# Superblock 0 ahead of superblock 1 in the head, weights issued behind GpSimd's products of superblock 1, and two output blocks in two steps each

## The chip, the core and the metric

The kernel runs on one core of one Trainium2 chip. A core has five engines with their own instruction queues: TensorE (PE in the profile, its weight loads PEld) for matrix products, VectorE (DVE), ScalarE (ACT) and GpSimd (POOL) for elementwise work, and SyncE (SP), which here only issues transfers. They meet through semaphores. The metric is the device time of one execution in microseconds; lower is better.

## What is computed

An RWKV-6 style recurrence over four batches of eight heads, 768 steps each, head size 48, whose output goes through an RMS norm and a gated feed-forward block (384 to 1536 to 384). Cut to what matters:

```python
# r, k, v, w: (4, 8, 768, 48); u: (8, 48)
state = 0                                   # (B, H, D, D)
for t in range(S):
    cur = einsum('bhd,bhe->bhde', u * k[t], v[t])
    y[t] = einsum('bhd,bhde->bhe', r[t], state + cur)
    state = w[t][..., None] * state + einsum('bhd,bhe->bhde', k[t], v[t])
x = y.transpose(0, 2, 1, 3).reshape(B * S, H * D)       # (3072, 384)
xn = x / sqrt(mean(x * x) + 1e-6) * rms_g
out = (silu(xn @ w_gate) * (xn @ w_val)) @ w_out        # 384 -> 1536 -> 384
```

## The kernel before

The 768 steps are cut into six superblocks of 128 steps. A step of the kernel is named fn.n.j: function, superblock n (0 to 5), and j, which is the batch (0 to 3) or, for the feed-forward steps, one of twelve blocks of 128 hidden units. Steps `load_gv.g.h` and `load_wo.g` take weight group g instead.

For each superblock and batch: `load_w`, `load_r`, `load_k`, `load_v` issue transfers on the sync queue (lines 247 to 261); `ln`, `cs_mm`, `exp_r`, `exp_k` make the running products of the decay w (logarithm on ACT, sums over steps on PE, exponentials on ACT); `r_mul` and `k_mul` scale r and k with them (lines 454 to 463; `k_mul` is on DVE in superblocks 0 and 1 and on POOL after that); `rk_pe` and `rk_tr` transpose the result (PE and an ACT copy in superblocks 0 and 1, a DMA transpose later); `q_mm` makes the 128x128 products of r and k, `q_mask_e`, `q_copy_o` and `q_mask_o` mask them; `bonus_mul` (two products on POOL, lines 467 and 468), `bonus_sum` (DVE) and `bonus_v` (POOL) make the term with u; `st_mm` and `st_new` carry the state; `x_pe`, `y_mm` or `y_mm`, `x_add` make y in PSUM; `x_sq`, `x_rstd`, `xn_mul`, `xn_pe`, `xn_out` are the norm and its transpose into `xnt`.

The feed-forward part of a superblock then takes twelve blocks of `gate_mm`, `val_mm` (three products of 512 columns each, line 626), `silu` (ACT) and `h_mul` (DVE, line 658), and four `o_mm` (twelve products of 384 columns each, line 672), `o_out` and `out_dma`. A hidden block's weights come from one of two tiles each for gate and value: group 0 holds blocks 0 to 3, group 1 blocks 4 to 11 (`GV = (0, 4, 12)`). The output weights `wo_sb` are one tile filled by three transfers of four blocks each (`load_wo.0` to `load_wo.2`, line 357). All weights are issued by POOL (lines 351 and 357), behind the POOL work that stands in front of them in the order.

The order of all work is written out by hand in the string `ORDER`: 1086 steps. Each engine runs its own steps in the order in which they stand there, and each queue its transfers. `warm` steps are products of zeros that PE does in the head, 36 of them.

PSUM has eight banks: two in ring "a" (gates, sums for r, y of even batches in superblock 0), two in ring "b" (values, sums for k, y of odd batches in superblock 0) and four in ring "q" (everything else). `psum` gives a new tile the bank of its ring whose last use stands earliest in `ORDER`, so the order of the steps also decides which bank a tile gets, and whom it waits for.

The next superblock's recurrence runs between the feed-forward blocks of the one before, so that PE has both to draw on; the head, up to the first `gate_mm.0.0`, has no feed-forward work to fill it.

Of the kernel before, what the change touches and what calls it, by code (L numbers as in the profile page):

```python
# [35 lines left out]
q_mm.0.2 load_r.2.0 q_mask_o.0.2 y_mm.0.1 bonus_mul.0.3 rk_tr.0.3 x_pe.0.0 q_mask_o.0.0 load_gv.0.0 q_mask_e.0.2
x_sq.0.1 cs_mm.1.1 y_mm.0.0 exp_r.1.1 load_w.2.3 bonus_v.0.2 warm.3.0 warm.20.0 bonus_sum.0.3 x_rstd.0.1 warm.15.0
x_sq.0.0 load_r.2.3 x_pe.0.2 y_mm.0.2 q_mm.0.3 warm.6.0 warm.14.0 xn_mul.0.1 bonus_v.0.3 warm.17.0 load_gv.0.1
x_rstd.0.0 r_mul.1.0 x_sq.0.2 warm.2.0 warm.33.0 warm.25.0 k_mul.1.0 xn_mul.0.0 load_gv.1.0 x_pe.0.3 warm.16.0
q_mask_e.0.3 q_mask_o.0.3 st_mm.0.0 warm.30.0 y_mm.0.3 exp_k.1.1 bonus_mul.1.0 bonus_mul.1.1 xn_pe.0.1 st_mm.0.3  # L40
x_rstd.0.2 st_new.0.0 warm.35.0 r_mul.1.1 warm.11.0 cs_mm.1.3 x_sq.0.3 warm.28.0 xn_pe.0.0 xn_out.0.1 xn_out.0.0
warm.0.0 st_new.0.3 xn_mul.0.2 x_rstd.0.3 exp_k.1.3 xn_mul.0.3 xn_pe.0.2 cs_mm.1.2 xn_out.0.2 xn_pe.0.3 xn_out.0.3
st_mm.0.2 rk_pe.1.0 st_mm.0.1 k_mul.1.1 exp_r.1.3 exp_r.1.2 st_new.0.2 exp_k.1.2 rk_tr.1.0 k_mul.1.3 gate_mm.0.0
val_mm.0.2 st_new.0.1 gate_mm.0.3 rk_pe.1.1 bonus_sum.1.0 silu.0.0 load_gv.1.1 val_mm.0.0 gate_mm.0.2 silu.0.3 silu.0.2
bonus_sum.1.1 rk_tr.1.1 h_mul.0.0 h_mul.0.2 r_mul.1.3 gate_mm.0.1 val_mm.0.3 gate_mm.0.9 silu.0.1 bonus_mul.1.3
val_mm.0.1 h_mul.0.3 silu.0.9 gate_mm.0.6 q_mm.1.0 bonus_sum.1.3 silu.0.6 gate_mm.0.7 q_copy_o.1.1 q_copy_o.1.0
q_mask_o.1.0 q_mask_o.1.1 gate_mm.0.5 rk_pe.1.3 bonus_v.1.0 h_mul.0.1 silu.0.7 val_mm.0.7 load_r.2.2 q_mask_e.1.0
load_wo.0.0 val_mm.0.6 q_mask_e.1.1 rk_tr.1.3 r_mul.1.2 gate_mm.0.11 k_mul.1.2 h_mul.0.7 cast_v.1.0 y_mm.1.0
load_wo.1.0 silu.0.5 cast_v.1.1 bonus_v.1.1 val_mm.0.9 rk_pe.1.2 h_mul.0.6 st_mm.1.0 st_mm.1.1 silu.0.11 val_mm.0.5
x_add.1.0 x_sq.1.0 h_mul.0.9 cast_v.1.2 val_mm.0.4 gate_mm.0.4 gate_mm.0.8 rk_tr.1.2 silu.0.4 st_new.1.0 st_new.1.1  # L50
q_mm.1.2 bonus_mul.1.2 load_wo.2.0 cast_v.1.3 q_copy_o.1.2 h_mul.0.5 silu.0.8 gate_mm.0.10 q_mask_o.1.2 h_mul.0.4
q_mask_e.1.3 val_mm.0.8 y_mm.1.1 st_mm.1.2 bonus_sum.1.2 q_copy_o.1.3 silu.0.10 bonus_v.1.3 st_mm.1.3 val_mm.0.11
q_mask_o.1.3 q_mask_e.1.2 h_mul.0.8 x_add.1.1 load_k.2.1 x_rstd.1.0 ln.2.0 x_sq.1.1 y_mm.1.3 h_mul.0.11 val_mm.0.10
bonus_v.1.2 x_add.1.3 y_mm.1.2 h_mul.0.10 x_rstd.1.1 x_add.1.2 xn_mul.1.0 x_sq.1.3 cs_mm.2.0 st_new.1.3 o_mm.0.0
x_rstd.1.3 ln.2.1 x_sq.1.2 load_v.2.1 xn_pe.1.0 cs_mm.2.1 ln.2.2 xn_mul.1.1 x_rstd.1.2 cs_add.2.0 xn_out.1.0 o_out.0.0
st_new.1.2 xn_mul.1.2 o_mm.0.2 cs_add.2.1 xn_pe.1.1 exp_r.2.0 r_mul.2.0 bonus_mul.2.0 exp_r.2.1 xn_pe.1.2 load_v.2.0
o_mm.0.1 w_tot.2.0 xn_out.1.2 cs_mm.2.2 exp_k.2.0 ln.2.3 xn_mul.1.3 w_tot.2.1 r_mul.2.1 load_k.2.2 load_k.2.3 exp_k.2.1
cs_mm.2.3 xn_out.1.1 xn_pe.1.3 cs_add.2.2 cs_add.2.3 k_mul.2.0 exp_r.2.2 o_mm.0.3 xn_out.1.3 k_mul.2.1 exp_r.2.3
cast_v.2.1 r_mul.2.2 bonus_mul.2.1 w_tot.2.2 o_out.0.2 exp_k.2.3 gate_mm.1.7 out_dma.0.0 val_mm.1.7 st_mm.2.1 rk_tr.2.0
exp_k.2.2 r_mul.2.3 w_tot.2.3 gate_mm.1.1 val_mm.1.1 k_mul.2.3 st_new.2.1 load_v.2.2 rk_tr.2.1 silu.1.7 gate_mm.1.5  # L60
k_mul.2.2 h_mul.1.7 silu.1.1 load_v.2.3 gate_mm.1.6 silu.1.5 val_mm.1.5 silu.1.6 h_mul.1.1 o_out.0.3 load_r.3.0
bonus_sum.2.1 load_w.3.1 bonus_mul.2.2 gate_mm.1.3 val_mm.1.6 o_out.0.1 gate_mm.1.0 h_mul.1.5 val_mm.1.0 bonus_sum.2.0
q_mm.2.0 silu.1.0 h_mul.1.6 cast_v.2.0 cast_v.2.2 val_mm.1.3 q_copy_o.2.0 q_mask_e.2.0 st_mm.2.0 q_copy_o.2.1 rk_tr.2.3
bonus_v.2.1 q_mask_o.2.0 h_mul.1.0 silu.1.3 st_new.2.0 q_mask_e.2.1 h_mul.1.3 gate_mm.1.2 st_mm.2.2 q_mask_o.2.1
silu.1.2 val_mm.1.2 y_mm.2.0 load_w.3.0 gate_mm.1.4 y_mm.2.1 gate_mm.1.10 bonus_v.2.0 rk_tr.2.2 h_mul.1.2 val_mm.1.4
silu.1.4 x_add.2.0 silu.1.10 x_add.2.1 st_new.2.2 gate_mm.1.9 gate_mm.1.8 val_mm.1.9 q_mm.2.2 h_mul.1.4 x_sq.2.1
x_sq.2.0 bonus_mul.2.3 load_r.3.1 silu.1.9 out_dma.0.3 gate_mm.1.11 cast_v.2.3 x_rstd.2.0 val_mm.1.11 x_rstd.2.1
load_k.3.0 bonus_sum.2.2 h_mul.1.9 q_mask_e.2.3 load_k.3.1 silu.1.8 load_v.3.0 q_copy_o.2.2 q_copy_o.2.3 q_mask_o.2.2
silu.1.11 ln.3.0 q_mask_e.2.2 load_w.3.3 q_mask_o.2.3 bonus_v.2.2 h_mul.1.11 load_w.3.2 ln.3.1 bonus_sum.2.3 st_mm.2.3
val_mm.1.10 y_mm.2.3 y_mm.2.2 val_mm.1.8 xn_mul.2.0 bonus_v.2.3 out_dma.0.2 h_mul.1.10 out_dma.0.1 load_r.3.3 cs_mm.3.0  # L70
x_add.2.2 h_mul.1.8 cs_add.3.0 o_mm.1.1 cs_mm.3.1 x_add.2.3 load_r.3.2 x_sq.2.2 load_v.3.2 load_k.3.2 st_new.2.3 ln.3.3
exp_r.3.0 x_sq.2.3 ln.3.2 x_rstd.2.2 w_tot.3.0 exp_k.3.0 xn_mul.2.2 xn_pe.2.0 xn_mul.2.1 cs_add.3.1 x_rstd.2.3 o_mm.1.0
xn_out.2.0 exp_r.3.1 exp_k.3.1 r_mul.3.0 o_out.1.0 k_mul.3.0 xn_pe.2.2 cs_mm.3.3 cs_add.3.3 k_mul.3.1 bonus_mul.3.1
w_tot.3.1 xn_mul.2.3 o_mm.1.3 rk_tr.3.0 xn_pe.2.1 xn_out.2.2 r_mul.3.1 bonus_mul.3.0 exp_r.3.3 o_out.1.1 out_dma.1.0
r_mul.3.3 cs_mm.3.2 cs_add.3.2 xn_pe.2.3 exp_k.3.2 rk_tr.3.1 w_tot.3.3 k_mul.3.2 exp_r.3.2 load_w.5.2 xn_out.2.3
xn_out.2.1 exp_k.3.3 r_mul.3.2 bonus_sum.3.1 load_k.4.2 o_out.1.3 o_mm.1.2 gate_mm.2.5 w_tot.3.2 val_mm.2.1
bonus_sum.3.0 o_out.1.2 bonus_v.3.0 cast_v.3.0 val_mm.2.0 cast_v.3.2 bonus_mul.3.2 out_dma.1.3 silu.2.5 gate_mm.2.0
q_mm.3.0 q_mask_e.3.0 load_k.3.3 silu.2.0 h_mul.2.0 load_v.3.1 gate_mm.2.1 silu.2.1 gate_mm.2.11 val_mm.2.5 h_mul.2.1
q_mask_e.3.1 silu.2.11 cast_v.3.1 rk_tr.3.2 st_mm.3.2 gate_mm.2.2 q_copy_o.3.0 k_mul.3.3 load_w.4.0 silu.2.2
q_copy_o.3.1 h_mul.2.5 st_new.3.2 q_mask_o.3.0 val_mm.2.2 gate_mm.2.3 gate_mm.2.4 st_mm.3.0 h_mul.2.2 silu.2.4  # L80
# [644 lines left out]
```

## Time and profile before

| what | us |
|---|---|
| median of three runs | 201.8 |
| lowest and highest run | 201.46, 202.18 |
| the profiled execution, in all | 201.61 |
| span of the profiled execution, first to last instruction | 199.9 |
| PE busy in the span | 192.6 |
| DVE, ACT, POOL busy | 151.6, 136.9, 125.5 |

How to read it: times in the timelines are from the start of the span. A row of a timeline has the start, the duration, the engine, the line of the kernel, the operation, output and inputs by the program's names, the shape and how many instructions were merged; in brackets stands the idle time before it and what ended it. PSUM tiles are named by ring and bank (ps_au, ps_qx). DMA rows show how many KB a transfer writes and the median time from issue to landing. Products on PE are pipelined, so the start of the next one, not the duration, tells what a product costs.

### The profile page before, as it was taken

Reading aid. Unit: us, or ns where it says so; the run is one execution under the profiler, and the core shown is the slowest. Engines: PE = TensorE matmul, PEld = TensorE weight load, DVE = VectorE, ACT = ScalarE, POOL = GpSimd, SP = SyncE. Lnnn points to the kernel's source line nnn. Section 1 sums busy time; section 2 is a strip of 40 time slices with the busy share of each in tenths; the row PEclk is TensorE's granted clock in tenths of the full one; section 3 lists DMA queues with packets and bytes.
Section 4 is the critical chain, followed back from the end, with each engine's and each line's share of the span. In section 5 each row is a group of like instructions: output and inputs, shape, how many; then the busy total and the mean of one; then the engine's idle time right before and its main releaser. Section 6 shows DMA issues by size and latency. Waiting matters only on the chain.

```text
span 199.9 us, 4406 instructions
## 1 busy us (share of the span) xinstructions
PE 192.6 (96%) x1577; PEld 113.7 (57%) x1577; DVE 151.6 (76%) x290; ACT 136.9 (69%) x279; POOL 125.5 (63%) x184
## 2 busy tenths in 40 slices
...
PEclk9999999999999999999999999999999999999999
...
GB/s 153 254 228 161 196 215 209 201 180 187 191 173 237 209 164 210 241 156 249 218 152 210 233 211 180 196 188 108 115 147 229 40 25 59 0 157 43 0 59 100
DMA packets 121566, 32.41 MB, mean 162 GB/s; under 512 B 116420, under 2 KB 120392, under 8 KB 121544
## 3 DMA queue, kind: packets, MB, share of 16 engines
...
q8 instruction: 12, 0.20, 0.4%
...
## 4 chain that ended last, share of the span: by engine, by line
PE 77%; SPq 6%; DMA 6%; DVE 5%; POOL 3%; issue 1%; ACT 0%; DVEq 0%
PE ps_av L626 10%; PE ps_bu L626 10%; PE ps_bv L626 10%; PE ps_au L626 10%; PE ps_qz L672 6%; PE ps_qu L672 6%; PE ps_qv L672 5%; PE ps_qx L672 5%; SPq L248 4%; DMA wo_sb<-in_moe_w_out_dram 4%; DMA kt<-in_k_dram 2%; SPq L261 2%; DVE rk L461 2%; POOL qts L520 1%; PE ps_bv L557 1%
## 5 line engine op out<-in xcount | busy, mean ns | idle before, releaser
L672 PEld LDWEIGHTS <-ht 128*128 128x128 bf16 x300 | 28.3, 98 | 17.3 <-issue 0.7
L235 ACT ACTIVATE sg<-ps_av 128x512 bf16<-128x512 f32 x37 | 22.2, 599 | 21.1 <-PE ps_av L626 18.5
L626 PEld LDWEIGHTS <-wg_sb 128*128 128x128 bf16 x216 | 23.0, 114 | 18.8 <-DVE wcol L451 0.2
L626 PEld LDWEIGHTS <-wv_sb 128*128 128x128 bf16 x216 | 22.8, 114 | 18.8 <-issue 0.9
L467 POOL TENSOR_TENSOR ruk<-rt,kt 128x384 f32<-128x384 f32 x24 | 24.4, 1016 | 9.9 <-DMA rt<-in_r_dram 5.0
L626 PE MATMUL ps_av<-xnt,wg_sb 128*128 128x512 bf16 x111 | 30.1, 380 | 0.0
L626 PE MATMUL ps_bu<-xnt,wv_sb 128*128 128x512 bf16 x108 | 29.3, 380 | 0.5 <-DVE ht L658 0.5
L658 DVE TENSOR_TENSOR ht<-ps_bu,sg 128x512 bf16<-128x512 f32 x36 | 24.7, 687 | 6.2 <-PE ps_bu L626 4.2
L658 DVE TENSOR_TENSOR ht<-ps_bv,sg 128x512 bf16<-128x512 f32 x36 | 24.7, 685 | 6.1 <-PE ps_bv L626 5.7
L626 PE MATMUL ps_bv<-xnt,wv_sb 128*128 128x512 bf16 x108 | 29.2, 379 | 0.0
L626 PE MATMUL ps_au<-xnt,wg_sb 128*128 128x512 bf16 x105 | 28.5, 380 | 0.0
L235 ACT ACTIVATE sg<-ps_au 128x512 bf16<-128x512 f32 x35 | 20.9, 596 | 9.7 <-PE ps_au L626 8.4
L468 POOL TENSOR_TENSOR ruk<-ruk,u_bc 128x384 f32<-128x384 f32 x24 | 24.2, 1009 | 1.9
L477 POOL TENSOR_TENSOR ydiag<-vt,diag 128x384 f32<-128x384 f32 x24 | 20.1, 842 | 1.1 <-DVE diag L472 1.1
L520 POOL TENSOR_SCALAR_AFFINE_SELECT qts<-qts 128x512 bf16<-128x512 bf16 x20 | 13.1, 663 | 11.9 <-ACT qts L513 11.8
L461 POOL TENSOR_TENSOR rk<-kt,ek 128x384 bf16<-128x384 f32 x16 | 15.9, 1006 | 1.7 <-DMA kt<-in_k_dram 0.9
L235 ACT ACTIVATE lw<-wt 128x384 bf16<-128x384 f32 (+1 forms) x20 | 11.3, 580 | 4.9 <-DMA wt<-in_w_dram 4.9
L233 ACT ACT_TABLE_LOAD x10 | 12.8, 1283 | 1.8 <-PEq L709 1.6
L672 PE MATMUL ps_qz<-wo_sb,ht 128*128 128x384 bf16 (+1 forms) x84 | 13.8, 314 | 0.0
L472 DVE TENSOR_REDUCE diag<-ruk 128x8 f32<-128x384 f32 x24 | 12.9, 542 | 0.7 <-POOL ruk L468 0.7
L672 PE MATMUL ps_qx<-wo_sb,ht 128*128 128x384 bf16 x72 | 12.8, 326 | 0.4 <-DMA wo_sb<-in_moe_w_out_dram 0.4
L672 PE MATMUL ps_qu<-wo_sb,ht 128*128 128x384 bf16 x72 | 12.7, 326 | 0.0
...
## 6 DMA issues: line engine op xcount, KB each, us to landing
rt<-in_r_dram SPq DMA_DIRECT2D x24, 192.0 KB, 3.8
kt<-in_k_dram SPq DMA_DIRECT2D x24, 192.0 KB, 4.0
vt<-in_v_dram SPq DMA_DIRECT2D x24, 192.0 KB, 3.8
out_dram<-ob SPq DMA_DIRECT2D x23, 192.0 KB, 2.6
wt<-in_w_dram SPq DMA_DIRECT2D x16, 192.0 KB, 3.7
wt<-in_w_dram SPq DMA_DIRECT2D x4, 384.0 KB, 4.5
wo_sb<-in_moe_w_out_dram POOLq DMA_DIRECT2D x3, 384.0 KB, 7.2
wg_sb<-in_moe_w_gate_dram POOLq DMA_DIRECT2D x1, 768.0 KB, 9.9
```

Of the source, the lines that this page charges most:

```text
L233: nc.scalar.preload_act_table_set(table_name)
L235: return nc.scalar.activation(**kw).ins
L248: dmas["load_" + which, n, j] = nc.sync.dma_start(out=inp[which, n, j], in_=t[j, :, n * L:(n + 1) * L, :].rearrange("h t d -> t h d")).ins
L461: eng.tensor_tensor(out=rk[:, n % 2, j, 1, :, 0:D], in0=inp["k", n, j], in1=bank["cs_k", n, j][:, 0:DM].rearrange("p (h d) -> p h d", h=H) ...
L467: nc.gpsimd.tensor_tensor(out=ruk[n, j], in0=inp["r", n, j], in1=inp["k", n, j], op=ALU.mult)
L468: nc.gpsimd.tensor_tensor(out=ruk[n, j], in0=ruk[n, j], in1=u_bc, op=ALU.mult)
L472: nc.vector.tensor_reduce(out=diag[n, j].rearrange("p h o -> p (h o)"), in_=ruk[n, j], axis=mybir.AxisListType.X, op=ALU.add)
L477: nc.gpsimd.tensor_tensor(out=ydiag[n, j], in0=inp["v", n, j], in1=diag[n, j].to_broadcast([128, H, D]), op=ALU.mult)
L520: nc.gpsimd.affine_select(out=qts[n, j][:, 1], in_=qts[n, j][:, 1], compare_op=ALU.is_gt, fill=0.0, base=0, pattern=[[0, NP], [1, 128]], c ...
L626: nc.tensor.matmul(ps[:, cols], lhsT=units(ws, c, f), rhs=xnt[n][:, c, cols], start=(first and c == 0), stop=(c == KC - 1))
L658: nc.vector.tensor_tensor(out=ht[n][:, f, :], in0=bank.pop(("v", n, f)), in1=bank.pop(("sg", n, f)), op=ALU.mult)
L672: nc.tensor.matmul(ps[:, cols], lhsT=ht[n][:, f, b * L:(b + 1) * L], rhs=wo_sb[:, f, cols], start=(f == 0), stop=(f == FC - 1))
```

## The change

Only the string `ORDER` and the output step change. The output step is split for two blocks, o.0.0 and o.0.2: `o_h` does the products of the first two weight groups (eight of twelve), and `o_mm` the rest (`o_h` is also entered in the table from which `psum` reads the last use of a bank):

```diff
+    def out_mm(n, j, fs):
+        b, cols = out_cols(n, j)
+        for f in fs:
+            nc.tensor.matmul(bank["o", n, j][:, cols], lhsT=ht[n][:, f, b * L:(b + 1) * L], rhs=wo_sb[:, f, cols],
+                             start=(f == 0), stop=(f == FC - 1))
+
+    def o_h(n, j):
+        bank["o", n, j] = psum("q", ("o", n, j), [128, DM])
+        out_mm(n, j, range(2 * FG))
+
     def o_mm(n, j):
-        b, cols = out_cols(n, j)
-        ps = bank["o", n, j] = psum("q", ("o", n, j), [128, DM])
-        for f in range(FC):
-            nc.tensor.matmul(ps[:, cols], lhsT=ht[n][:, f, b * L:(b + 1) * L], rhs=wo_sb[:, f, cols],
-                             start=(f == 0), stop=(f == FC - 1))
+        done = 2 * FG if ("o", n, j) in bank else 0
+        if not done:
+            bank["o", n, j] = psum("q", ("o", n, j), [128, DM])
+        out_mm(n, j, range(done, FC))
```

Engine by engine, the new order differs from the old one only in the head and around the first output blocks:

- PE: 30 `warm` steps instead of 36. q_mm.0.2 goes ahead of x_pe.0.1; y_mm.0.0 and q_mm.0.3 ahead of cs_mm.1.1; x_pe.0.3, y_mm.0.3 and xn_pe.0.1 ahead of st_mm.0.0; gate_mm.0.0 and gate_mm.0.3 ahead of st_mm.0.1 and val_mm.0.2. Later, o_h.0.0, o_h.0.2 and xn_pe.1.0 go ahead of what is left of o_mm.0.0.
- DVE: q_mask_o.0.0 goes ahead of k_mul.0.3; q_mask_e.0.3 and q_mask_o.0.3 ahead of r_mul.1.0 and k_mul.1.0; xn_out.0.1 ahead of st_new.0.0; r_mul.1.1 behind xn_out.0.3 and st_new.0.2; h_mul.0.0 ahead of bonus_sum.1.0 and bonus_sum.1.1; st_new.1.2 ahead of cs_add.2.0.
- ACT: rk_tr.0.3 ahead of cast_v.0.2; xn_mul.0.3 ahead of exp_k.1.3; exp_k.1.2 ahead of exp_r.1.2; silu.0.0 ahead of rk_tr.1.0; xn_mul.1.3 ahead of exp_r.2.1.
- POOL and its queue: the two products bonus_mul.1.0 go ahead of the transfers load_gv.0.1 (value weights of group 0) and load_gv.1.0 (gate weights of group 1).
- SP: load_r.2.0, load_r.2.1 and load_w.2.3 go ahead of load_k.2.0.

The lines of the new order that hold the two places:

```diff
+load_k.2.0 x_rstd.0.1 bonus_v.0.2 x_sq.0.0 bonus_v.0.3 r_mul.1.0 x_pe.0.2 warm.24.0 load_r.2.3 warm.25.0 warm.26.0
...
+xn_mul.0.1 k_mul.1.0 y_mm.0.2 x_rstd.0.0 x_pe.0.3 x_sq.0.2 y_mm.0.3 bonus_mul.1.0 load_gv.0.1 load_gv.1.0 xn_mul.0.0
...
+cs_mm.2.0 st_new.1.3 o_h.0.0 o_h.0.2 st_new.1.2 x_rstd.1.3 ln.2.1 x_sq.1.2 load_v.2.1 xn_pe.1.0 o_mm.0.0 cs_mm.2.1
```

More of the change, by code (lines that the diff above doesn't have):

```diff
@@ L36 @@
[L36 to L80, printed above, removed]
@@ new lines @@
+xn_pe.0.1 st_mm.0.0 warm.27.0 xn_out.0.1 st_new.0.0 exp_k.1.1 x_rstd.0.2 xn_pe.0.0 st_mm.0.3 cs_mm.1.3 x_sq.0.3
+xn_out.0.0 st_new.0.3 xn_mul.0.2 warm.28.0 xn_pe.0.2 rk_pe.1.0 warm.29.0 st_mm.0.2 x_rstd.0.3 xn_out.0.2 bonus_mul.1.1
+load_gv.1.1 xn_mul.0.3 st_new.0.2 exp_k.1.3 exp_r.1.3 xn_pe.0.3 cs_mm.1.2 exp_k.1.2 exp_r.1.2 xn_out.0.3 r_mul.1.1
+gate_mm.0.0 gate_mm.0.3 k_mul.1.1 st_mm.0.1 val_mm.0.2 silu.0.0 rk_pe.1.1 k_mul.1.3 rk_tr.1.0 st_new.0.1 val_mm.0.0
+gate_mm.0.2 silu.0.3 silu.0.2 rk_tr.1.1 h_mul.0.0 bonus_sum.1.0 bonus_sum.1.1 h_mul.0.2 r_mul.1.3 gate_mm.0.1
```

152 lines of the change are left out of this document (94 added, 58 removed).

## The prediction

> **What bounds the kernel now.** I read the page's slices first, where the granted clock of TensorE is full in all 40, then stretches of the run, then TensorE's waits, and only then the timelines of the places where those waits lie.
>
> ```profile
> PEclk9999999999999999999999999999999999999999
> ```
>
> ```profile
> 55.00:197.00 142.00, 141.93 (x1112) 83.66 (x1110) 108.19 (x207) 94.23 (x193) 88.82 (x129) 1.00 0.72 149
> ```
>
> The columns are the stretch, its length, the busy time of PE, PEld, DVE, ACT and POOL, then the granted clock, the DMA share and GB/s. From 55 to 197 us PE is busy 141.93 of 142 us: that part is a fixed list of products. The change leaves it alone, so the end moves only by as much as PE reaches 55 us earlier or later.
>
> ```profile
> PE ps_bv L557 <- DVE rk L461: 1.1, 1, 1.1
> ...
> PE ps_bu L626 <- DVE ht L658: 0.5, 1, 0.5
> PE ps_qx L672 <- DMA wo_sb<-in_moe_w_out_dram: 0.4, 1, 0.4
> ```
>
> These are PE's own waits (us in total, times, longest). After the start-up only two stand between the first gate product and the end; each has its place in PE's timeline:
>
> ```profile
> 19.41 0.88 PE L557 MATMUL ps_bv<-ydiag,ident 128*128 128x384 f32 x2 [1.10 <-DVE rk L461]
> ...
> 31.12 0.81 PE L626 MATMUL ps_au<-xnt,wg_sb 128*128 128x512 bf16 x3
> 31.77 0.81 PE L626 MATMUL ps_bv<-xnt,wv_sb 128*128 128x512 bf16 x3
> ...
> 33.06 0.61 PE L484 MATMUL ps_qv<-ident,rk 128*128 128x128 bf16 x8
> 33.51 0.81 PE L626 MATMUL ps_bu<-xnt,wv_sb 128*128 128x512 bf16 x3
> ...
> 36.09 0.81 PE L626 MATMUL ps_bu<-xnt,wv_sb 128*128 128x512 bf16 x3 [0.47 <-DVE ht L658]
> 36.74 0.81 PE L626 MATMUL ps_au<-xnt,wg_sb 128*128 128x512 bf16 x3
> ...
> 41.09 0.81 PE L626 MATMUL ps_bu<-xnt,wv_sb 128*128 128x512 bf16 x3
> ```
>
> ```profile
> 52.45 1.46 PE L672 MATMUL ps_qx<-wo_sb,ht 128*128 128x384 bf16 x8
> 54.35 0.81 PE L672 MATMUL ps_qx<-wo_sb,ht 128*128 128x384 bf16 x4 [0.44 <-DMA wo_sb<-in_moe_w_out_dram]
> ...
> 57.71 2.11 PE L672 MATMUL ps_qu<-wo_sb,ht 128*128 128x384 bf16 x12
> 59.66 0.33 PE L417 MATMUL ps_au<-lw,mask_lt 128*128 128x384 bf16 x1
> ```
>
> At 31.12 is gate_mm.0.0, at 31.77 val_mm.0.2, at 36.09 val_mm.0.3, at 36.74 gate_mm.0.9, the first product on the second gate tile, and at 41.09 val_mm.0.7, the first on the second value tile. A gate or value block takes 31.77 - 31.12 = 0.65 us of issue, rk_pe 33.51 - 33.06 = 0.45. Twelve output products take 59.66 - 57.71 = 1.95, so eight take 1.30.
>
> **Part 1, the output blocks: -0.60 us.** Today PE stands from 52.45 + 1.30 = 53.75 to 54.35 because o_mm.0.0 needs the third wo tile. Afterwards o_h.0.0 and o_h.0.2 issue sixteen products (2.60 us) that need only the first two tiles, so PE comes back to the third tile at 52.45 + 2.60 plus the transposes, 55.2, with the data there since 54.3. The number of products is the same. Two PSUM banks are held instead of one; the allocator gives them those of y.1.3 and y.1.2, and xn_pe.1.0 the one of st.1.3.
>
> ```profile
> 52.69 0.55 DVE L561 TENSOR_TENSOR xb<-ps_qz,ydiag 128x384 f32<-128x384 f32 x1
> ...
> 53.74 0.56 DVE L537 TENSOR_TENSOR st<-ps_qv,wcol 128x384 bf16<-128x384 f32 x1
> ```
>
> The x_add that frees y.1.2 ends at 53.24, before PE wants it at 53.75; st.1.3 is free at 54.30, before 55.05. Bounds: 0 (something else holds PE there) to 0.60; I take all of it, since both frees have 0.5 us or more.
>
> **Part 2, superblock 0 first in the head: gate_mm.0.0 about 1.1 us earlier, but not the work behind it.** The even and odd masks of block 3 now precede superblock 1's r and k products on DVE, q_mask_o.0.0 fills DVE's wait for k, and xn_mul.0.3 precedes exp_k.1.3 on ACT.
>
> ```profile
> 27.24 0.49 ACT L570 ACTIVATE junk<-ps_bv 128x384 bf16<-128x384 f32 x1 [0.77 <-PE ps_bv L552]
> ...
> 28.62 0.47 ACT L235 ACTIVATE ek<-ps_bu 128x384 f32<-128x384 f32 x1
> 28.99 0.57 ACT L585 ACTIVATE xn<-ps_bv,rstd 128x384 bf16<-128x384 f32 x1
> ```
>
> x_sq.0.3 loses its wait of 0.77 for y_mm.0.3, and xn_mul.0.3 the 28.99 - 28.62 = 0.37 of exp_k.1.3: 1.14 us. Everything after it up to gate_mm.0.0 hangs on it, so gate_mm.0.0 moves from 31.12 to about 30.0. The earlier silu.0.0 and h_mul.0.0 also take away the wait of 0.47 at 36.09. Six warm-up products fewer cost nothing by themselves: they fill time in which PE would stand.
>
> **Part 3, the weights later: this decides the head.** The value tile of group 0 and the gate tile of group 1 are now issued behind bonus_mul.1.0.
>
> ```profile
> 21.79 0.84 POOL L477 TENSOR_TENSOR ydiag<-vt,diag 128x384 f32<-128x384 f32 x1
> 23.53 1.07 POOL L477 TENSOR_TENSOR ydiag<-vt,diag 128x384 f32<-128x384 f32 x1 [0.91 <-DVE diag L472]
> 24.55 0.81 POOL L351 DMA_DIRECT2D wv_sb<-in_moe_w_val_dram  x1
> 25.36 0.78 POOL L351 DMA_DIRECT2D wg_sb<-in_moe_w_gate_dram  x1
> 26.15 1.01 POOL L467 TENSOR_TENSOR ruk<-rt,kt 128x384 f32<-128x384 f32 x1
> 27.24 1.00 POOL L468 TENSOR_TENSOR ruk<-ruk,u_bc 128x384 f32<-128x384 f32 x1
> 28.19 1.31 POOL L467 TENSOR_TENSOR ruk<-rt,kt 128x384 f32<-128x384 f32 x1
> ...
> 30.52 0.80 POOL L351 DMA_DIRECT2D wv_sb<-in_moe_w_val_dram  x1
> ```
>
> ```profile
> 27.31 1.34 DVE L455 TENSOR_TENSOR rk<-rt,er 128x384 bf16<-128x384 f32 x1
> ```
>
> ```profile
> wg_sb<-in_moe_w_gate_dram POOLq DMA_DIRECT2D x1, 768.0 KB, 9.9
> wv_sb<-in_moe_w_val_dram POOLq DMA_DIRECT2D x1, 768.0 KB, 9.4
> ...
> wv_sb<-in_moe_w_val_dram POOLq DMA_DIRECT2D x1, 384.0 KB, 6.3
> ```
>
> The pair of products takes 28.19 - 26.15 = 2.04 us. Against it, bonus_v.0.3 loses most of its wait of 0.91 for DVE's sum, which no longer stands behind q_mask_o.0.0: it starts right behind bonus_v.0.2, at about 22.6, and lasts 0.8. The pair then starts at 23.4, and the value tile is issued at 25.45, 0.9 us later than today. But DVE's two products of superblock 1 with both inputs in SBUF now fall on this pair: the row at 27.31 takes 1.34 because it stands until POOL's product ends, and POOL's next takes 1.31 instead of 1.01. That is 0.3 us for each of two, so the delay is between 0.9 and 1.5 us; I take 1.3, as at least one of the two must meet.
>
> Landings by the rows today: value tile 24.55 + 6.3 = 30.85, gate tile 25.36 + 9.9 = 35.26, second value tile 30.52 + 9.4 = 39.92. All three go through one queue in order, and that queue is nearly alone while it has packets: in the two microseconds from 28 the other queue moved none.
>
> ```profile
> ## 3 DMA queue, kind: packets, MB, share of 16 engines
> q0 software_dynamic: 347, 0.40, 119.1%
> ```
>
> So I let the landings move with the issue: value tile 32.15, gate tile 36.56. PE does gate_mm.0.0 and 0.3 from 30.0 to 31.3, st_mm.0.1 (four small products, about 0.2), and then stands until 32.2 for val_mm.0.2. Behind it come rk_pe.1.1 and five blocks: 0.45 + 5 x 0.65 = 3.70, so gate_mm.0.9 could issue at 35.9, but its weights land at 36.56. It issues at 36.6 instead of 36.74: **-0.15 us**. With a delay of 0.9 it is -0.55, with 1.5 it is +0.05; if the tile's last packets gain because the next transfer is now queued right behind, the chain's 35.9 bounds it at -0.85. The second value tile lands by about 40.4, in front of its use at 40.9.
>
> Two rules of the Trainium skill bear on this, "DMA: Bandwidth & Descriptors". Its section "Queues, rings and completion order" has each engine round-robin between queues packet by packet; the row above shows the small-packet queue getting none for 2 us, so an even share does not hold here. Its section "Anatomy of one DMA — SWDGE (gpsimd) path" prices a transfer at 2.0 us plus bytes over 436 GB/s, an estimate of 2.9 us for the value tile where the trace has 6.3; by that page no weight would be late and the head would give the result of the first rival below.
>
> **Part 4, loads of superblock 2.** The r loads go ahead of k on the sync queue, and k.2.0 goes three loads back, to the issue at 54.79.
>
> ```profile
> 54.79 0.70 SPq L261 DMA_DIRECT2D wt<-in_w_dram  x1
> ```
>
> ```profile
> 57.98 1.00 POOL L467 TENSOR_TENSOR ruk<-rt,kt 128x384 f32<-128x384 f32 x1 [2.75 <-DMA rt<-in_r_dram]
> ...
> 61.62 1.00 POOL L461 TENSOR_TENSOR rk<-kt,ek 128x384 bf16<-128x384 f32 x1 [0.60 <-DMA kt<-in_k_dram]
> ```
>
> ```profile
> wt<-in_w_dram SPq DMA_DIRECT2D x16, 192.0 KB, 3.7
> ```
>
> k.2.0 lands at 54.79 + 3.7 = 58.5 and POOL's product starts 0.5 us later than 57.98; the wait of 0.60 before k_mul.2.1 absorbs that. Cost 0. Without this cover 0.5 us would reach st_mm.2.1.
>
> **Sum.** -0.60 - 0.15 = -0.75 us on the span of 199.9, so 199.15; the profiled execution took 201.61 in all, so 200.86. The median shown, 201.8 (201.46 to 202.18), is 0.2 above that execution; I forecast **200.9**. With the bounds of parts 1 and 3 its own range is 200.1 to 201.7.
>
> **Rivals.** (1) *The weights don't hold PE*: then the order alone counts, gate_mm.0.9 issues at 30.0 + 1.30 + 0.2 + 3.70 = 35.2, which is -1.55, with part 1 -2.15: 199.5. For it: the queue would have to be quicker than today's rows of 6.3 and 9.9; nothing shows that. Chance 0.10.
> (2) *The gain is given back after 55 us*: the loads of superblock 2 come at DMA's pace, not PE's. The row at 61.62 shows one stage bound by its load. That product ends at 62.62, and its user on PE stands at 63.60, so 0.9 us can be used up before PE waits; 0.75 just fits. If all is lost: 201.6. Chance 0.15.
> (3) *The weights come too late*, slower: if bonus_v.0.3 gains nothing and the pair meets DVE twice, the issue is 2.04 + 0.6 = 2.65 us later, the gate tile lands at 37.9 and gate_mm.0.9 is 1.2 us late; less part 1, +0.6: 202.2. It decides from a delay of about 2.1 us on, where the head's loss equals part 1's gain. For it: the weights have no slack to spare (36.74 - 35.26 = 1.48). Against it: the sum that bonus_v.0.3 needs is moved forward by one mask operation on DVE. Chance 0.20.
> The forecast itself keeps 0.55.
>
> **Numbers.** 0.3%, 0.6 us, is about what a measurement of this kernel can tell from no change. Of the forecast's 0.55 some 0.42 lie beyond -0.6 us and 0.13 within; with rival 1, faster is 0.52; same 0.13 + 0.15 = 0.28; slower 0.20. The range 199.8 to 202.1 leaves out rival 1's end and the far end of rival 3.
>
> **What would show it.** Right: no wait for wo_sb on PE; eight products of ps_qx, then eight of another bank; the first gate product near 30.0, and then a PE wait for the DMA of wv_sb near 31.4 and one for wg_sb before the first product of the second tile, near 36.6. The value tile's issue on POOL near 25.9. Wrong: no wait for weights at all (rival 1), a new PE wait behind 55 us (rival 2), or an issue on POOL near 27 (rival 3). An idle stretch of PE at 31.4 that also lowered the granted clock would break the sum; the wait of 1.10 at 19.41 did not lower it: the slices read 9 throughout.

## The result: no change, and the profile after

| | before | changed |
|---|---|---|
| median, 22 runs each | 201.78 | 201.75 |
| lowest and highest run | 200.34, 204.03 | 200.65, 203.64 |
| profiled execution | 201.61 | 201.21 |
| its span | 199.9 | 199.5 |

The ratio is 1.0007, with a 95% interval of 0.9984 to 1.0030: no change that the measurement can tell. The forecast was 200.9, its range 199.8 to 202.1. The profiled execution of the changed kernel is one of its quicker ones (the sixth of 22): it lies 0.54 below its median, that of before 0.17 below its own. So most of the 0.4 us by which the changed kernel's trace is shorter can lie in which executions were profiled.

PE's own waits in the changed kernel (us in total, times, longest). Those for the third tile of wo and for ht are gone; one for a value tile and one for GpSimd's cast of v (vb) are new:

```profile
PE ps_bv L625 <- DMA wv_sb<-in_moe_w_val_dram: 0.6, 1, 0.6
PE ps_au L625 <- DVE xnt L606: 0.3, 1, 0.3
PE ps_qv L529 <- POOL vb L380: 0.3, 1, 0.3
```

Their places in PE's timeline, changed kernel:

```profile
30.25 0.81 PE L625 MATMUL ps_au<-xnt,wg_sb 128*128 128x512 bf16 x3 [0.31 <-DVE xnt L606]
30.90 0.81 PE L625 MATMUL ps_av<-xnt,wg_sb 128*128 128x512 bf16 x3
31.55 0.33 PE L529 MATMUL ps_qu<-vb,rk 128*128 128x96 bf16 x4
32.46 0.84 PE L625 MATMUL ps_bv<-xnt,wv_sb 128*128 128x512 bf16 x3 [0.58 <-DMA wv_sb<-in_moe_w_val_dram]
...
35.52 0.81 PE L625 MATMUL ps_bu<-xnt,wv_sb 128*128 128x512 bf16 x3
36.44 0.84 PE L625 MATMUL ps_au<-xnt,wg_sb 128*128 128x512 bf16 x3
...
52.18 1.46 PE L670 MATMUL ps_qx<-wo_sb,ht 128*128 128x384 bf16 x8
53.48 1.46 PE L670 MATMUL ps_qz<-wo_sb,ht 128*128 128x384 bf16 x8
54.77 0.33 PE L595 MATMUL ps_qv<-ident,xn 128*128 128x128 bf16 x3
54.94 0.81 PE L670 MATMUL ps_qx<-wo_sb,ht 128*128 128x384 bf16 x4
...
61.43 0.81 PE L625 MATMUL ps_au<-xnt,wg_sb 128*128 128x512 bf16 x3
62.08 0.81 PE L625 MATMUL ps_bv<-xnt,wv_sb 128*128 128x512 bf16 x3
63.19 0.33 PE L529 MATMUL ps_qv<-vb,rk 128*128 128x96 bf16 x4 [0.30 <-POOL vb L380]
...
195.36 1.15 PE L670 MATMUL ps_qu<-wo_sb,ht 128*128 128x192 bf16 x12
```

The rows of before for the last two stretches:

```profile
62.31 0.81 PE L626 MATMUL ps_au<-xnt,wg_sb 128*128 128x512 bf16 x3
62.95 0.81 PE L626 MATMUL ps_bv<-xnt,wv_sb 128*128 128x512 bf16 x3
63.60 0.33 PE L530 MATMUL ps_qx<-vb,rk 128*128 128x96 bf16 x4
...
195.78 1.15 PE L672 MATMUL ps_qz<-wo_sb,ht 128*128 128x192 bf16 x12
```

Four starts make an account: gate_mm.0.0, the first output product, gate_mm.1.7, the last group of products. Changed minus before they are 30.25 - 31.12 = **-0.87**, 52.18 - 52.45 = **-0.27**, 61.43 - 62.31 = **-0.88** and 195.36 - 195.78 = **-0.42**. So the head gains 0.87, the stretch up to the output blocks loses 0.60, the split of the output blocks gains 0.61, and the rest loses 0.46. All of that 0.46 is at st_mm.2.1: it could issue at 62.08 + 0.65 = 62.73 and stands until 63.19. (The bracket counts only the part that the weight load also waited.) GpSimd's timeline shows why:

```profile
58.67 1.00 POOL L466 TENSOR_TENSOR ruk<-rt,kt 128x384 f32<-128x384 f32 x1 [3.71 <-DMA kt<-in_k_dram]
59.74 0.99 POOL L467 TENSOR_TENSOR ruk<-ruk,u_bc 128x384 f32<-128x384 f32 x1
60.69 2.00 POOL L460 TENSOR_TENSOR rk<-kt,ek 128x384 bf16<-128x384 f32 x2
62.63 0.51 POOL L380 CAST vb<-vt 128x384 bf16<-128x384 f32 x1
```

GpSimd stands 3.71 us for k.2.0, then runs bonus_mul.2.0, k_mul.2.0, k_mul.2.1 and cast_v.2.1 without a pause, up to 63.14. Before, the same cast ran from 62.56 to 63.06, also too late for a PE that comes at 62.73, but then PE came at 63.60.

The late start at 58.67 is hardly what holds the cast, though. k_mul.2.1, the second of the two products at 60.69, also needs the load of k.2.1. SyncE's issue of it and its time from issue to landing (lowest, median, highest of one), changed kernel and then before:

```profile
57.55 0.81 SPq L247 DMA_DIRECT2D kt<-in_k_dram  x1
DMA to landing us min/median/max: 4.0/4.0/4.0
...
57.73 0.64 SPq L248 DMA_DIRECT2D kt<-in_k_dram  x1
DMA to landing us min/median/max: 3.8/3.8/3.8
```

It landed at 61.6 and 61.5. Before, k_mul.2.1 began 0.1 later, at 61.62; in the changed kernel it began at 60.69 + 1.00 = 61.69, again 0.1 later. GpSimd was through with its earlier work just as k.2.1 came, so an earlier start would have left the cast about where it is.

### The profile page after: what moved, and what is told of

Same layout as the page of the kernel before. It is cut to its first block, busy times and chain, and to the rows that moved or that the text cites. A ratio compares the mean times of both kernels' runs of the same rounds, so it can differ in the third digit from the quotient of the medians.

```text
span 199.5 us, 4394 instructions
## 1 busy us (share of the span) xinstructions
PE 193.5 (97%) x1571; PEld 114.0 (57%) x1571; DVE 150.7 (76%) x290; ACT 136.9 (69%) x279; POOL 125.0 (63%) x184
## 3 DMA queue, kind: packets, MB, share of 16 engines
HBM read 25.96 MB, written 4.72 MB: 154 GB/s over the span
## 4 chain that ended last, share of the span: by engine, by line
PE 68%; SPq 10%; DMA 10%; POOL 7%; issue 2%; ACT 0%; DVE 0%; POOLq 0%
PE ps_av L625 11%; PE ps_bu L625 10%; PE ps_bv L625 10%; PE ps_au L625 10%; SPq L247 7%; PE ps_qu L670 5%; DMA wg_sb<-in_moe_w_gate_dram 5%; PE ps_qv L670 5%; PE ps_qx L670 5%; PE ps_qz L670 4%; DMA kt<-in_k_dram 4%; SPq L260 3%; POOL ruk L467 2%; POOL ruk L466 1%; POOL ydiag L476 1%
## 5 line engine op out<-in xcount | busy, mean ns | idle before, releaser
L670 PE MATMUL ps_qx<-wo_sb,ht 128*128 128x384 bf16 x84 | 15.0, 326 | 0.0
L670 PE MATMUL ps_qu<-wo_sb,ht 128*128 128x384 bf16 (+1 forms) x84 | 13.8, 314 | 0.0
L584 ACT ACTIVATE xn<-xb,rstd 128x384 bf16<-128x384 f32 x20 | 11.8, 608 | 1.2 <-POOL rstd L579 1.2
## 6 DMA issues: line engine op xcount, KB each, us to landing
wg_sb<-in_moe_w_gate_dram POOLq DMA_DIRECT2D x1, 768.0 KB, 10.4
```

The lines of the kernel that those rows point to most:

```text
L670: nc.tensor.matmul(bank["o", n, j][:, cols], lhsT=ht[n][:, f, b * L:(b + 1) * L], rhs=wo_sb[:, f, cols], start=(f == 0), stop=(f == FC - 1))
```

## The experiments

All times are on the chip, with before run beside them. For each trace I read the same four starts (us):

| kernel | gate_mm.0.0 | first output | gate_mm.1.7 | last group | ratio to before, 95% interval |
|---|---|---|---|---|---|
| before | 31.12 | 52.45 | 62.31 | 195.78 | |
| changed | 30.25 | 52.18 | 61.43 | 195.36 | 1.0007 (0.9984 to 1.0030) |
| e1 split alone | 31.20 | 52.53 | 61.79 | 195.24 | 0.9994 (0.9976 to 1.0012) |
| e2 head alone | 30.25 | 51.84 | 61.29 | 196.67 | 1.0024 (1.0000 to 1.0049) |
| e3 weights early | 31.06 | 52.03 | 61.28 | 195.43 | 0.9993 (0.9969 to 1.0016) |
| e4 state later | 29.75 | 51.27 | 60.62 | 194.82 | 1.0004 (0.9982 to 1.0025) |
| e5 both | 31.27 | 52.24 | 61.49 | 195.65 | 0.9996 (0.9970 to 1.0023) |
| e6 k first | 31.13 | 52.14 | 61.40 | 194.86 | one run, 200.68 us |
| e7 clear | 29.86 | 50.91 | 60.80 | 194.42 | 0.9974 (0.9947 to 1.0000) |
| e8 state first | 30.57 | 51.55 | 60.80 | 195.97 | 1.0048 (1.0017 to 1.0078) |
| e9 weights later | 29.85 | 56.24 | 65.49 | 198.96 | 1.0226 (1.0192 to 1.0261) |
| e10 GpSimd's order | 30.11 | 51.34 | 60.59 | 195.96 | 1.0029 (1.0004 to 1.0055) |
| e11 the same, old head | 31.90 | 53.23 | 62.49 | 196.35 | 1.0033 (1.0003 to 1.0063) |
| e12 loads | 30.04 | 51.10 | 60.82 | 194.59 | 0.9995 (0.9972 to 1.0017) |

The eleven kernels with the new head have gate_mm.0.0 between 29.75 and 31.27, mean 30.38; the three with the old one at 31.12, 31.20 and 31.90, mean 31.41. The first difference among the changed kernel, e3, e4 and e5 in any engine's order stands at 23 us, and still their q_mm.0.2 begins at 19.18, 19.99, 18.68 and 20.19; from there to gate_mm.0.0 all four take 11.07 or 11.08. So a single trace starts up to 1.5 us early or late, and a difference in the last group must be read against the first start.

**e1: the split of the output blocks alone.** Before's order up to cs_mm.2.0, the changed one behind it.

> Only the two output blocks in two steps, with the old head. Theory (the time saved at the output blocks is real, and what was lost behind them is a new wait of the state product st_mm.2.1 for GpSimd's cast_v.2.1): no wait of PE for wo_sb, gate_mm.1.7 near 61.7 instead of 62.31, st_mm.2.1 held by about 0.1 us at most because the old order of the loads lets cast_v.2.1 end at 63.06; span 199.4, 0.5 below before. Rival (the end does not follow PE's place at 63 us, but the loads): span 199.9, as before.

The wait for wo is gone, the first output product to gate_mm.1.7 takes 61.79 - 52.53 = 9.26 instead of 9.86, and the last group comes 0.54 earlier. Nothing of it is lost behind 62 us. The median is 200.97 beside 201.13; the interval reaches from -0.5 to +0.2 us, so the time alone does not prove it.

**e2: the new head alone.** The changed order up to cs_mm.2.0, before's behind it.

> The changed kernel's order up to cs_mm.2.0 and the order of before from there on, so o_mm.0.0 is one step again and waits for the third block of wo_sb. Theory A (what the head gains is lost at that wait, since wo_sb lands when GpSimd's issue lets it): weights' waits of 0.5 to 0.9 us near 32 and 36 us, o_mm.0.0 begins at 51.7 to 52.9, the wait for wo_sb grows from 0.44 to between 0.6 and 0.9 us, no wait over 0.2 us at st_mm.2.1; last product 196.2 to 196.7, span 199.5 to 199.9, ratio 0.998 to 1.000. Rival B (the gain of the head adds up with nothing behind it): wait for wo_sb as before, last product 196.1 or less with gate_mm.0.0 at 30.6 or earlier.

Both theories missed. The first output product comes 0.61 earlier than before and the wait at wo shrinks to 0.2, but the end is 0.89 later. PE's waits in e2:

```profile
PE ps_qu L502 <- DVE ht L658: 0.5, 1, 0.5
PE ps_qz L502 <- DMA rkT<-rk: 0.4, 1, 0.4
...
PE ps_qx L530 <- POOL vb L381: 0.3, 1, 0.3
...
104.70 0.09 PEld L502 LDWEIGHTS <-rkT 48*128 48x128 bf16 x1 [0.67 <-DMA rkT<-rk]
```

Besides 0.44 us at st_mm.2.1 PE now stands before 77.2 and before 104.7, both times for a transpose by DMA. The first row names VectorE's h_mul for the second of these waits, but the weight load of the same product, in the last row, waits for the transpose, and VectorE had last read the bank ps_qu at 101.0 to 101.6. The profiled run (202.49) is one of the slower of its twelve, but the median, 201.63, is above before too.

**e3, e4, e5, e7: one wait after the other taken away.** e3 issues the weights ahead of bonus_mul.1.0 again; e4 moves st_mm.2.1 back; e5 does both; e7 also moves st_new.2.1.

```diff
-y_mm.0.3 bonus_mul.1.0 load_gv.0.1 load_gv.1.0 xn_mul.0.0      (e3, e5, e7)
+y_mm.0.3 load_gv.0.1 load_gv.1.0 bonus_mul.1.0 xn_mul.0.0
-val_mm.1.7 st_mm.2.1 ... gate_mm.1.1 val_mm.1.1                (e4, e5, e7)
+val_mm.1.7 ... gate_mm.1.1 val_mm.1.1 st_mm.2.1
-k_mul.2.3 st_new.2.1 ... silu.1.6 h_mul.1.1                    (e7)
+k_mul.2.3 ... silu.1.6 h_mul.1.1 st_new.2.1
```

> The changed kernel with the weights of value group 0 and gate group 1 issued ahead of bonus_mul.1.0 again. Theory (the weights hold the head, and behind 62 us the cast of v holds PE whatever the head does): PE no longer waits for wv_sb at 31.7, the first product on the second gate tile moves from 36.4 to about 35.7; but st_mm.2.1 stays near 63.2, its wait grows from 0.46 to about 1.1, and the span stays within 0.2 of the changed kernel's 199.5. Rival (the head sets the end): span 198.8.

> The changed kernel with one step moved: st_mm.2.1 stands behind gate_mm.1.1 and val_mm.1.1 instead of in front of them. Theory (the 0.46 us in front of st_mm.2.1 are what ate half of the gain): that wait is gone, span 199.05, 0.45 below the changed kernel and 0.85 below before. Rival (PE meets the next late load instead): span 199.5.

> Both of the above: weights ahead of bonus_mul.1.0, st_mm.2.1 behind val_mm.1.1. Theory: the head's 0.7 us now reach the end, span 198.3 to 198.5, about 1.5 us below before, ratio of times 0.992 to 0.993. Rival (the loads of superblock 2 set the pace further on): span 199.0 to 199.5.

> The changed kernel with the weights issued early again (load_gv.0.1 and load_gv.1.0 ahead of bonus_mul.1.0), st_mm.2.1 behind val_mm.1.1 on TensorE and, new, st_new.2.1 behind h_mul.1.1 on VectorE. Theory A (the end is TensorE's chain from its first gate product, fixed in length, plus the waits in it): from gate_mm.0.0 to the last product it takes 164.6 us plus its waits (changed kernel: 30.25 to 196.27 with waits of 0.58, 0.27 and 0.46; st_mm.2.1 moved alone: 29.75 to 195.73 with 0.5 and 0.7). Here neither the weights nor the state's products hold it, nor does h_mul stand behind the state on VectorE, so no wait over 0.2 us is left behind 30 us: last product 164.5 to 164.9 us behind gate_mm.0.0, which comes at 29.7 to 31.3 as the first loads fall; span 197.6 to 199.2, median time 199.7 to 200.4, ratio 0.993 to 0.997. Rival B (each wait taken away comes back at the next place, as with both moves before): another wait of 0.5 to 0.8 us between 60 and 75 us, last product 165.1 us or more behind gate_mm.0.0, ratio 0.998 to 1.001.

The weights' waits go in e3: gate_mm.0.0 to the first output product takes 20.97 us, against 21.93 in the changed kernel. But the wait at st_mm.2.1 grows to 0.68. In e4 and e5 that wait is gone and a new one of 0.7 stands one place on, since VectorE's st_new.2.1 now holds the h_mul behind it; the row is PE's wait in e5:

```profile
PE ps_bv L626 <- DVE ht L658: 0.6, 1, 0.6
```

So the end that was expected of e5 did not come. In e5 the cast ended at 62.17, before PE could have come to st_mm.2.1 in its old place (62.14 + 0.65 = 62.79), so there the move only cost. e4's span, 198.9, lies near the 199.05 expected of it, but by luck: its head began 0.50 earlier than the changed kernel's, and from gate_mm.0.0 to the last group it takes 165.07 us, the changed kernel 165.11. e7 clears the wait of 0.7 too, and again one appears, this time earlier, at gate_mm.1.7. PE's timeline and VectorE's, e7:

```profile
60.80 0.84 PE L626 MATMUL ps_au<-xnt,wg_sb 128*128 128x512 bf16 x2 [0.47 <-DVE wcol L451]
...
60.12 0.55 DVE L455 TENSOR_TENSOR rk<-rt,ps_au 128x384 bf16<-128x384 f32 x1 [0.61 <-DMA rt<-in_r_dram]
60.59 0.16 DVE L451 TENSOR_TENSOR wcol<-ps_au,half_of 128x8 f32<-128x8 f32 x1
```

gate_mm.1.7 needs the bank that r_mul.2.2 and w_tot.2.2 still read, and these wait for the load of r.2.2. e7 has the earliest end of all traces, and 0.9974 the lowest ratio, but from gate_mm.0.0 to the last group it still takes 194.42 - 29.86 = 164.56 us, against 163.73 in e6 below. Its interval touches 1.

**e12: two loads of superblock 2 earlier.** e7 with

```diff
-load_w.2.2 load_r.2.0 ... load_k.2.0 ... load_r.2.3 ... load_r.2.2
+load_w.2.2 load_k.2.0 load_r.2.0 ... load_r.2.2 ... load_r.2.3
```

> The kernel with the weights early and the state's steps moved back (median ratio 0.9974, last wait 0.64 us at gate_mm.1.7, whose bank VectorE held while it waited 0.61 us for a load of r), with two loads of superblock 2 put elsewhere on SyncE: load_k.2.0 ahead of load_r.2.0 again, as in the kernel before, and load_r.2.2 ahead of load_r.2.3. Theory A (the lead of the head is lost where SyncE's loads of superblock 2 come late, and their order decides where): GpSimd's first product of superblock 2 begins at 55 to 57 us instead of 57.9, cast_v.2.1 ends at 61.0 to 62.5, VectorE waits 0.3 us or less for r.2.2, gate_mm.1.7 waits 0.3 us or less; last group 163.7 to 164.1 us behind gate_mm.0.0; median ratio 0.9945 to 0.9975. Rival B (the loads as a whole come at the pace of the transfers, and some later one takes the place: r.2.3, k.2.1 or v.2.1): a wait of 0.4 us or more between 59 and 66 us, last group 164.3 us or more behind gate_mm.0.0, ratio 0.997 to 1.000.

r.2.2 holds nothing any more. Now it is w.2.3, which k.2.0 put one load back and ScalarE's ln.2.3 needs. ScalarE's timeline and PE's, e12:

```profile
57.87 0.52 ACT L235 ACTIVATE lw<-wt 128x384 bf16<-128x384 f32 x1 [0.84 <-DMA wt<-in_w_dram]
...
58.44 0.32 PE L417 MATMUL ps_av<-lw,mask_lt 128*128 128x384 bf16 x1 [0.32 <-ACT lw L235]
...
60.82 0.81 PE L626 MATMUL ps_au<-xnt,wg_sb 128*128 128x512 bf16 x2
```

cs_mm.2.3 stands 0.46 us, gate_mm.1.7 comes at 60.82 as in e7, and the ratio is 0.9995. The loads that were moved came as theory A said (GpSimd's first product begins at 55.03, the cast ends at 62.34, gate_mm.1.7 does not wait), but the end is rival B's: 164.55 us from gate_mm.0.0 to the last group, with the new wait a little ahead of the place given.

**e6: only k.2.0 ahead of the r loads again**, the changed kernel otherwise.

```diff
-load_w.2.2 load_r.2.0 ... load_k.2.0
+load_w.2.2 load_k.2.0 load_r.2.0 ...
```

> The changed kernel with load_k.2.0 back ahead of load_r.2.0 on SyncE, nothing else. Theory A (the three loads behind which k.2.0 was put do not set cast_v.2.1, since k.2.1 and v.2.1 stand behind the same loads either way; the wait at st_mm.2.1 comes because TensorE is earlier, not because GpSimd is later): GpSimd's first product of superblock 2 begins up to 0.8 us earlier, cast_v.2.1 still ends at 62.0 to 63.2, and st_mm.2.1 waits as before it, 0.2 to 0.7 us with gate_mm.0.0 at 30.0 to 30.7. Rival B (that move made GpSimd late): cast_v.2.1 ends 0.5 us or more before st_mm.2.1 is reached, no wait there.

GpSimd's timeline and PE's, e6:

```profile
55.49 1.00 POOL L467 TENSOR_TENSOR ruk<-rt,kt 128x384 f32<-128x384 f32 x1 [0.57 <-DMA rt<-in_r_dram]
...
60.94 1.00 POOL L461 TENSOR_TENSOR rk<-kt,ek 128x384 bf16<-128x384 f32 x1 [2.03 <-DMA kt<-in_k_dram]
61.89 0.50 POOL L381 CAST vb<-vt 128x384 bf16<-128x384 f32 x1
...
62.69 0.33 PE L530 MATMUL ps_qv<-vb,rk 128*128 128x96 bf16 x4
```

bonus_mul.2.0 begins 3.2 us earlier than in the changed kernel, and the cast ends at 62.39 instead of 63.14, now set by the load of k.2.1 alone. st_mm.2.1 comes to it at 62.69 and does not wait; the changed kernel's PE, at 62.73, would not have waited either. Neither expectation fits whole: the cast ends where theory A has it, and there is no wait, as rival B has it, but by 0.30 us instead of 0.5. And that the move made the cast earlier is not shown. k.2.1 was issued at 57.09 and landed at 60.8, 0.7 earlier than in the changed kernel. In e4, e5 and e7, where k.2.0 has the changed kernel's late place, k.2.1 landed at 60.8, 60.3 and 60.7, and the cast ended at 62.34, 62.17 and 62.37. One run can't be told from this spread.

It is also the cleanest trace of all: its head is 0.88 later than the changed kernel's, no wait over 0.2 us is left behind gate_mm.0.0, and its last group is 0.50 earlier.

**e8 and e10: GpSimd's state steps first.** e3 with k.2.0 behind v.2.1, and on GpSimd

```diff
-bonus_mul.2.0 k_mul.2.0 k_mul.2.1 cast_v.2.1 bonus_mul.2.1 k_mul.2.3 k_mul.2.2 bonus_mul.2.2 cast_v.2.0
+k_mul.2.1 cast_v.2.1 k_mul.2.0 bonus_mul.2.1 bonus_mul.2.0 k_mul.2.3 k_mul.2.2 bonus_mul.2.2 cast_v.2.0
```

In e10 bonus_mul.2.2 stands behind q_mask_o.2.1 as well.

> The changed kernel with the weights issued early again, load_k.2.0 behind load_v.2.1 on SyncE, and on GpSimd k_mul.2.1, cast_v.2.1 and k_mul.2.0 ahead of bonus_mul.2.1 and bonus_mul.2.0; the order of TensorE and VectorE is the changed kernel's. Theory A (st_mm.2.1 waits because GpSimd comes to cast_v.2.1 only after two steps of bonus_mul.2.0 and both k_mul, and the loads of k.2.1 and v.2.1 are behind k.2.0's): cast_v.2.1 ends at 61.2 to 62.3 instead of 63.1, st_mm.2.1 waits at most 0.3 us, last product 164.6 to 164.9 us behind gate_mm.0.0, ratio 0.993 to 0.997. Rival B (the loads come at the pace of the transfers, whatever stands ahead of them): k.2.1 and v.2.1 land no earlier, cast_v.2.1 ends at 62.4 or later, the wait of 0.4 to 0.7 us stays, ratio 0.998 to 1.001. Rival C: k.2.0, now later, holds something: a wait at q_mm.2.0, or of VectorE at bonus_sum.2.1 and so of TensorE on ht.

> The kernel with GpSimd's state steps first (k.2.0 behind v.2.1, weights early), and bonus_mul.2.2 put behind q_mask_o.2.1 on GpSimd, so that cast_v.2.0 no longer stands behind it. Theory A (TensorE's chain of 163.7 us from gate_mm.0.0 to the start of its last group, plus waits; the only wait of the run with the state steps first was 1.7 us at st_mm.2.0, behind bonus_mul.2.2 and cast_v.2.0): that wait falls to 0.3 us or less, none over 0.3 us behind 30 us, start of the last group 163.6 to 164.1 us behind gate_mm.0.0, median 199.8 to 200.5 on a chip where before has 201.0, ratio 0.993 to 0.9975. Rival B (GpSimd is full from 59 us on, what is put back there comes late at the next place: bonus_sum.2.2 and h_mul behind it, or q_mask_o): another wait of 0.5 us or more between 70 and 85 us, ratio 0.998 or more.

In e8 the cast ends at 61.17 and st_mm.2.1 goes at 62.10 without a wait. But GpSimd had stood 5.06 us for k.2.1 and still had the two products of bonus_mul.2.0 to do, so cast_v.2.0 comes late, and st_mm.2.0 stands 1.7 us, to 71.10. PE's wait in e8:

```profile
PE ps_qv L530 <- POOL vb L381: 1.5, 1, 1.5
```

e10 takes that wait away, and the loss spreads over four places between 61 and 78 us, of 0.35 to 0.46 each: rival B. Both kernels are slower than before, by 0.5% and 0.3% in the median ratio, with intervals clear of 1.

**e11: the old head under the same rest.** e10 with before's order up to cs_mm.2.0.

> The same kernel with the head of before (superblock 1 in front, its weights and loads), up to cs_mm.2.0, load_k.2.0 behind load_v.2.1 in both; so the pair differs by the change's head alone, with no wait at wo_sb or at the states behind it. Theory A (the new head is worth what the traces show: gate_mm.0.0 at 29.8 to 31.3, 30.4 in the mean of eight profiles, instead of 31.1 and 31.2, and the wait of 0.64 us at val_mm.0.3 gone, less 0.25 us of products that now stand behind gate_mm.0.0): 0.9 to 1.4 us slower than its partner, ratio to before 0.998 to 1.001. Rival B (the new head's gain is spread away by the first loads and by the loads of superblock 2, so that head against head is worth nothing in time): within 0.4 us of its partner, or faster.

gate_mm.0.0 comes at 31.90 instead of 30.11, and the last group at 196.35 instead of 195.96: of a lead of 1.79 us in the traces 0.39 arrive. The medians are 201.57 for the old head and 201.72 for the new: rival B, head against head worth nothing that twelve runs each can tell. By their spread, an estimate, the difference is known to about 0.7 us, so a gain of a few tenths is not excluded.

**e9: the weights later still.**

```diff
-y_mm.0.3 bonus_mul.1.0 load_gv.0.1 load_gv.1.0 ... xn_out.0.2 bonus_mul.1.1 load_gv.1.1
+y_mm.0.3 bonus_mul.1.0 ... xn_out.0.2 bonus_mul.1.1 load_gv.0.1 load_gv.1.0 load_gv.1.1
```

> The changed kernel with load_gv.0.1 and load_gv.1.0 behind bonus_mul.1.1 as well, so that the three weight tiles are issued in a row behind two blocks' products: their issue falls 2.8 to 3.0 us later than in the changed kernel (about 28.0 and 28.8 us). Theory A (landing follows the issue, 6.3 to 7.3 us for the value tile and 9.9 to 10.4 us for the gate tile, and TensorE waits for the value tile at val_mm.0.2): the value tile lands at 34.3 to 35.6, TensorE waits 2.4 to 3.6 us there, with up to 0.5 us at gate_mm.0.9; the wait of 0.46 us at st_mm.2.1 is gone since TensorE comes there later than GpSimd, which is not held; so the end is 2.0 to 3.4 us later than the changed kernel's: median time 203.2 to 204.8, ratio 1.010 to 1.017. Rival B (the transfer is quicker when it is issued later, because the loads of superblock 1 are out of the way): landing 3 to 4 us behind the issue, wait of 0.5 us or less, ratio 0.999 to 1.003.

GpSimd issues the value tile at 29.40, later than expected because bonus_mul.1.1 itself waited 2.01 us for k. It lands 6.0 us later, as theory A has it. PE's timeline, then its stretches (columns as in the prediction: busy time of PE, PEld, DVE, ACT, POOL, then the granted clock, DMA share, GB/s), e9:

```profile
31.14 0.33 PE L530 MATMUL ps_qu<-vb,rk 128*128 128x96 bf16 x4
35.42 1.47 PE L626 MATMUL ps_bv<-xnt,wv_sb 128*128 128x512 bf16 x3 [3.95 <-DMA wv_sb<-in_moe_w_val_dram]
36.69 1.06 PE L484 MATMUL ps_qv<-ident,rk 128*128 128x128 bf16 x8
```

```profile
35.30:38.30 3.00, 2.88 (x13) 1.59 (x14) 0.00 (x0) 0.00 (x0) 0.00 (x0) 0.50 1.13 202
38.30:40.00 1.70, 1.70 (x9) 0.90 (x8) 1.15 (x3) 0.57 (x2) 0.00 (x0) 0.99 1.11 198
```

The wait lasts 3.95 us, and for three more the clock is halved (eight transposes take 1.06 us instead of 0.61), which theory A had not counted. The median of its six runs is 4.6 us above before.

## Why the prediction came out as it did

The time lies in the range, 0.85 above the forecast. That range also held no change at all, so the time alone says little for the sum; the gain of 0.75 us was not measured. Step by step, in the traces:

- **Part 1, -0.60: right.** 9.86 to 9.25 us in the changed kernel, 9.26 in e1.
- **Part 2, gate_mm.0.0 about 1.1 us earlier: right.** 30.25 in the trace, 1.03 us earlier in the means of eleven and of three traces, which spread by 1.5 and 0.8. The wait of 0.47 for ht has gone as well.
- **Part 3, gate_mm.0.9 at 36.6 after waits for both tiles: near in the sum by luck, since both of its factors were wrong and the errors cancelled.** It came at 36.44, behind stands of 0.74 for the value tile and 0.27 for the gate tile. GpSimd's timeline:

```profile
22.95 0.99 POOL L466 TENSOR_TENSOR ruk<-rt,kt 128x384 f32<-128x384 f32 x1 [0.67 <-DMA kt<-in_k_dram]
24.02 1.19 POOL L467 TENSOR_TENSOR ruk<-ruk,u_bc 128x384 f32<-128x384 f32 x1
25.16 0.81 POOL L350 DMA_DIRECT2D wv_sb<-in_moe_w_val_dram  x1
25.96 0.77 POOL L350 DMA_DIRECT2D wg_sb<-in_moe_w_gate_dram  x1
```

  The issue moved by 0.61, not 1.3: the pair of products began at 22.95, not 23.4, and only one of the two took longer (1.19). But the transfers were slower than the rows of before, which I had let move with the issue. The changed kernel's transfers, issue to landing, and its queues from 28 to 30 us:

```profile
wg_sb<-in_moe_w_gate_dram POOLq DMA_DIRECT2D x1, 768.0 KB, 10.4
wv_sb<-in_moe_w_val_dram POOLq DMA_DIRECT2D x1, 384.0 KB, 7.3
...
q0 software_dynamic: 313, 0.31, 100.2%
q1 hardware_dynamic: 215, 0.04, 14.0%
```

  In the stretch in which the weight queue had been alone, the sync queue's loads now took a share. Issue plus landing time is 25.16 + 7.3 = 32.5 for the value tile and 25.96 + 10.4 = 36.4 for the gate tile, where I had 32.15 and 36.56. Other executions with the weights in this place do not repeat it. In e4, whose order is the changed kernel's up to 62 us, the tiles took 5.9 and 9.7 us, and PE stood 0.52 for the gate tile alone; in e6, whose head came 0.88 later, they took 5.4 and 9.7, and PE stood for neither. So whether the weights hold PE, the premise of this part, differs from execution to execution.
- **Part 4, cost 0: right, in this trace.** I let the wait of 0.60 before k_mul.2.1 absorb a start that is 0.5 later. GpSimd started 0.7 later, 58.67 instead of 57.98, and that wait was used up; but k.2.1, landing at 61.6, would have held the product to about 61.69 anyway, against 61.62 before. The cast ended 0.08 later.
- **Rival 2, dismissed up to a loss of 0.9 us: the step that failed.** I set the slack from the end of k_mul.2.1, 62.62, to its user on PE at 63.60. The same user also needs cast_v.2.1, which the trace of before has from 62.56 to 63.06. So the slack was 63.60 - 63.06 = 0.54. PE came 0.87 earlier, at 62.73, so at least 0.33 had to come back; with the cast 0.08 later, and 0.05 from its end to the start of the product, it was 0.46. The rival's cause, loads of superblock 2 that don't come earlier when PE does, stands behind this wait (k.2.1 at 61.5 before and 61.6 now) and behind those of e7 (r.2.2) and e12 (w.2.3).
- **Rivals 1 and 3 did not happen in the changed kernel's trace.** e3 and e9 bracket the change: with the value tile issued 1.6 us earlier PE waits for no weights, with it 4.2 us later it waits 3.95. But in e6 the weights, in the changed kernel's place, did not hold PE, as rival 1 has it.

So in the trace -0.42 instead of -0.75. That the medians show -0.03 is not settled: the interval reaches to -0.3 only, the places of the two profiled executions below their medians differ by 0.37, and the kernels with the earliest ends that were run more than once (e7, e12, e4, e1) have ratios of 0.9974 to 1.0004. What the traces show is that PE, with the new head, stands for something that hangs on the loads of superblock 2: 0.46 us at st_mm.2.1 in the changed kernel, 0.68 there in e3, 0.64 at gate_mm.1.7 in e7, 0.46 at cs_mm.2.3 in e12. A late head is no guard against it: e3's begins at 31.06 and e6's at 31.13, but e6 does not stand there, as k.2.1 landed at 60.8 in e6 and at 61.5 in e3. In e2, e8 and e10 more is lost behind the head than it gained, to transposes and to GpSimd's order. Which of this the unprofiled runs went through no trace can tell.
